# Fused attention and a four-expert mixture: the second stage's query tiles start at 0, 64, 192, 320 and 448

## The chip, the cores and the metric

One Trainium2 chip, one core. The metric is the device time of one execution in microseconds (us). A program is launched once; its inputs and its output lie in the chip's memory (HBM).

## What is computed

Eight batches of 576 tokens. The first stage is an attention with eight heads of width 64 (heads 0 to 3 look at the last 32 tokens, heads 4 to 7 at every 32nd token). Its result x (576 x 512 in each batch) goes to the second stage: four experts, each a causal attention over all 576 tokens with a head of width 64, and for each token the two experts with the largest gate value are summed with their weights.

```python
logits = x @ w_gate
topk = np.argpartition(-logits, K, axis=-1)[..., :K]      # K = 2 of 4 experts
w = np.exp(sel - max); w /= w.sum()
for e in range(4):
    q, k, v = x @ wq[e], x @ wk[e], x @ wv[e]
    scores = (q @ k.T) / 8, keys after the query masked
    a = softmax(scores)
    out += (w of expert e, 0 where not chosen) * (a @ v @ wo[e])
```

## The kernel before

Experts go in pairs: `ep` is 0 or 1, and `a` (0 or 1) is the expert within the pair. Expert a of a pair lies in partitions 64a to 64a+63 of the projected queries and keys, so that the two experts' score products run side by side in the two halves of TensorE's rows.

Each operation of the program is made by `op(kind, engines, key, fn, r, w, mode)`. The operations are numbered in the order in which they are made (2573 of them), and `schedule()` issues them in the order of the written list `ORDER`. `SECOND` names those that go to the second of their allowed engines (ScalarE or VectorE for copies), and `FILL` puts idle 128-column products ahead of some early operations. TensorE thus works through its operations in the order of that list, and waits wherever an operand isn't there. `mode` is the way in which the array is divided for an operation; TensorE's operations have these:

- 128x128: projections (`pj`, L906 and L918), values (`vp`, L853), output products (`yp`, L1110), scores of the short tile (`s2_4`, L972)
- 64x128 (two halves of the rows): scores (`s2`, L992), transposes of the probabilities (`t2`, L1048)
- 128x64 (two halves of the columns): probabilities by values (`acc`, L1081)
- 64x32, 64x64 and 32x64: the first stage's products (L628, L642, L736, L755) and one small product of the gate (`gate4`, L836)

`attend(b, ep, qk, un, key)` does one pair of experts of one batch for one of two units of query tiles. The tiles start at 0, 128, 256, 384 and 512; unit 0 has the first three, unit 1 the fourth and the fifth, which is 64 queries tall. For a tile of 128 queries: `s2` makes the scores against all keys up to the tile's end, as three products for each expert (high by high, low by high, high by low parts); `max2` (VectorE) masks, finds the maximum and writes the scores to SBUF; `exp2` (ScalarE) exponentiates and sums; after the unit's last tile, `recip2` (VectorE) takes reciprocals, and `scale2` (GpSimd) multiplies the probabilities by reciprocal and gate weight. The 64-row tile holds both experts in one 128-row tile: `qd` is a block-diagonal copy of its queries, `s2_4` makes 576 columns in two products of 288 columns each (three passes each), and `scale2_4` scales them. `t2` then transposes 64 x 128 blocks (50 of these in the two units of a pair: 12 + 12, 8 + 8 + 10), `t2_out` copies them from PSUM to `th` (10 copies), and `acc` multiplies them with the values: 768 columns for each expert in unit 0, 832 in unit 1. `oh` and `ol` split the sum into two parts. `out_tile` makes one 128 x 512 tile of the output from both pairs (six products of 512 columns), copies it and stores it.

The first stage (`stage1`) and the second stage of different batches are interleaved by `ORDER`. Units 1 of an even batch and of the odd one after it are done late, after both have units 0.

Of the kernel before, what the change touches and what calls it, by code (L numbers as in the profile page):

```python
# [20 lines left out]
def attention_moe_kernel(  # L21
# [28 lines left out]
    QT = [(0, 128), (128, 128), (256, 128), (384, 128), (512, 64)]  # L50
    UNITS = [[0, 1, 2], [3, 4]]
    NT = len(QT)
    HS = S // 2
    NV = E * D + E
# [26 lines left out]
    class Ring:  # L81
# [32 lines left out]
    }  # L114
    ORDER = [
# [242 lines left out]
    for m in (m_loc, m_str, m_cau, m_last):  # L358
        nc.vector.memset(m, 0.0)
# [15 lines left out]
    for hf in range(2):  # L375
        keep(m_last[64 * hf:64 * hf + 64, HS - 64:], [[-1, 64]], 0, 1)

# [816 lines left out]
```

## Time and profile before

| what | value |
|---|---|
| time, median of 3 runs | 445.7 us (442.08 to 446.44) |
| profiled execution: time | 446.46 us |
| profiled execution: span of the core's instructions | 444.7 us |
| mean granted TensorE clock in the span | 0.992 |
| TensorE matmuls busy | 427.8 us (96% of the span) |
| VectorE / ScalarE / GpSimd busy | 345.9 / 269.5 / 221.0 us |

The profiled execution is at the upper end of the three timed runs, 0.76 us above their median; 1.76 us of its time lie outside the span. Busy time is the union of the instructions' times on an engine. A matmul's time is from its issue to its last result, so consecutive ones overlap: what one costs is read from the starts of two that follow each other, not from its duration.

### The profile page before, as it was taken

To read this page: it belongs to the slowest core of one execution; us is meant where nothing else is said; L and a number is where in the kernel's file an instruction comes from. 1 tells how busy PE (TensorE), PEld (TensorE's weight loads), DVE (VectorE), ACT (ScalarE), POOL (GpSimd) and SP (SyncE) were. 2 spreads that over 40 slices of the span, in tenths; PEclk is the share of its full clock that TensorE was granted. 3 is DMA by queue.
4 is the path that set the end of the run, shared out by engine and by line. 5 is a ranking of instruction groups with operands and counts; after the bars stand their busy time and mean duration, and the time that the engine had idled before them with its cause. 6 is when DMAs were issued, how large, how long until landed. Compare 5 with 4: busy or idle time off the path is not lost.

```text
span 444.7 us, 19093 instructions
## 1 busy us (share of the span) xinstructions
PE 427.8 (96%) x7716; PEld 382.8 (86%) x7716; DVE 345.9 (78%) x1104; ACT 269.5 (61%) x848; POOL 221.0 (50%) x408
## 2 busy tenths in 40 slices
PE   7899998999989999999999999999999999999996
PEld 6788987977879998997889898998879998998874
DVE  6878899889985977789997768796998868555651
ACT  4475537676675757556486475557565577645662
POOL 4556641777534633376536552346833754405440
PEclk9989999999999999999999999999999999999999
DMA  6756656636545604545625336215832211001113
GB/s 178 188 140 151 126 116 125 125 58 107 113 103 118 124 23 105 113 90 118 117 50 131 68 59 124 61 33 107 193 76 73 67 43 54 1 1 58 45 68 118
DMA packets 156272, 41.89 MB, mean 94 GB/s; under 512 B 145976, under 2 KB 149432, under 8 KB 156184
## 3 DMA queue, kind: packets, MB, share of 16 engines
q1 hardware_dynamic: 156184, 40.67, 41.3%
q8 instruction: 61, 1.00, 0.9%
q14 instruction: 27, 0.22, 0.2%
HBM read 31.20 MB, written 9.44 MB: 91 GB/s over the span
## 4 chain that ended last, share of the span: by engine, by line
PE 85%; DVE 4%; SPq 3%; issue 3%; DMA 2%; ACT 2%; POOL 1%; POOLq 0%; DVEq 0%; ACTq 0%
PE bank L906 20%; PE bank L1110 12%; PE bank L853 10%; PE bank L1081 9%; PE bank L992 7%; PE bank L1048 6%; PE bank L736 4%; PE bank L972 3%; PE bank L755 3%; PE bank L628 3%; PE bank L642 3%; DMA v<-in_v_dram 1%; PE bank L706 1%; PE bank L816 1%; SPq L549 1%
## 5 line engine op out<-in xcount | busy, mean ns | idle before, releaser
L1029 POOL TENSOR_SCALAR p<-p,st,wt 128x512 f32<-128x512 f32 (+3 forms) x128 | 76.6, 610 | 42.4 <-DVE st L1013 17.2
L1004 ACT ACTIVATE p<-p,st 128x384 f32<-128x384 f32 (+3 forms) x128 | 71.8, 569 | 0.7 <-DVE st L999 0.6
L999 DVE CUSTOM_DVE_ANT_0 p<-bank,m_cau 128x128 f32<-128x128 f32 (+3 forms) x128 | 57.2, 481 | 6.6 <-PE bank L992 5.7
L927 ACT CAST qk<-bank 128x288 fp32r<-128x288 f32 x64 | 25.2, 400 | 56.3 <-PE bank L906 49.8
L338 ACT COPY th<-bank 128x384 f32<-128x384 f32 (+2 forms) x119 | 46.1, 436 | 13.5 <-PE bank L1048 9.8
L523 DVE STREAM_TRANSPOSE qkt<-nat 128x576 f32<-128x576 f32 x48 | 47.7, 1006 | 1.5 <-DMA nat<-in_k_dram 1.2
L1081 PE MATMUL bank<-th,vs 128*64 128x192 f32 (+4 forms) x512 | 48.5, 337 | 0.0
L1081 PEld LDWEIGHTS bank<-th,vs 128*64 128x64 f32 x512 | 33.6, 137 | 13.9 <-issue 6.9
L718 ACT CAST xh<-bank 128x128 fp32r<-128x128 f32 (+4 forms) x112 | 28.7, 322 | 21.6 <-PE bank L736 10.4
L720 DVE TENSOR_TENSOR xl<-bank,xh 128x128 fp32r<-128x128 f32 (+4 forms) x112 | 32.1, 324 | 12.4 <-ACT xh L718 11.7
L929 DVE TENSOR_TENSOR qkl<-bank,qk 128x288 fp32r<-128x288 f32 x64 | 27.8, 444 | 12.6 <-ACT qk L927 12.5
L1048 PE MATMUL bank<-ident,p 64*128 64x64 f32 x800 | 36.5, 226 | 0.5 <-DVE xl L720 0.3
L853 PE MATMUL bank<-wl_v,xh 128*128 128x260 f32 x128 | 36.2, 283 | 0.6 <-issue 0.6
L1048 PEld LDWEIGHTS bank<-ident,p 64*128 64x128 f32 x800 | 32.3, 139 | 5.3 <-issue 1.6
L853 PE MATMUL bank<-wh_v,xh 128*128 128x260 f32 x128 | 36.4, 284 | 0.0
L853 PE MATMUL bank<-wh_v,xl 128*128 128x260 f32 x128 | 36.2, 283 | 0.0
L906 PE MATMUL bank<-xh,wh_k 128*128 128x288 f32 x120 | 36.1, 301 | 0.0
L906 PE MATMUL bank<-xh,wh_q 128*128 128x288 f32 x120 | 35.9, 299 | 0.0
L906 PE MATMUL bank<-xl,wh_k 128*128 128x288 f32 x120 | 35.8, 299 | 0.0
L906 PE MATMUL bank<-xh,wl_k 128*128 128x288 f32 x120 | 35.8, 298 | 0.0
L906 PE MATMUL bank<-xl,wh_q 128*128 128x288 f32 x120 | 35.7, 298 | 0.0
L906 PE MATMUL bank<-xh,wl_q 128*128 128x288 f32 x120 | 35.5, 296 | 0.0
(182 smaller groups left out, 1254.4 us busy)
## 6 DMA issues: line engine op xcount, KB each, us to landing
out_dram<-ys SPq DMA_DIRECT2D x32, 256.0 KB
nat<-in_q_dram SPq DMA_DIRECT2D x96, 72.0 KB
nat<-in_k_dram SPq DMA_DIRECT2D x96, 72.0 KB
v<-in_v_dram SPq DMA_DIRECT2D x96, 40.0 KB
v<-in_v_dram SPq DMA_DIRECT2D x48, 54.0 KB
v<-in_v_dram SPq DMA_DIRECT2D x32, 48.0 KB
v<-in_v_dram SPq DMA_DIRECT2D x32, 45.0 KB
out_dram<-ys SPq DMA_DIRECT2D x8, 128.0 KB
```

What stands on the lines that cost most here:

```text
L338: (nc.scalar.copy if e == "ACT" else nc.vector.tensor_copy)(dst, src)
L523: op("tq", {"DVE": 0.66 if local else 1.11}, k0 - 13, lambda e, x=x: nc.vector.transpose(turned(qkt.t, x), raw(x) if local else raw(x).rea ...
L720: op("xl", {"DVE": dve(n_)}, key + 0.5, lambda e, s_=s_, x_=x_: nc.vector.tensor_sub(x_(xl.t), s_(xa.t), x_(f(xh.t))), r=[xa, xh[u]], w=[x ...
L853: nc.tensor.matmul(vp.t[:, :NV], xx.t[:, t0:t0 + 128], ww.t[:, kt, :], start=i == 0, stop=i == 11)
L906: nc.tensor.matmul(pj.t[:, :HS], ww.t[:, kt, ep * 128:(ep + 1) * 128], xx.t[:, c], start=i == 0, stop=i == 11)
L992: nc.tensor.matmul(sp[a].t[:, :nk], x.t[r, 0, q0:q0 + 128], y.t[r, 1, :nk], start=i == 0, stop=i == 2)
L999: lambda e, sp=sp, p=p, a=a, nk=nk, ci=ci: nc.vector.tensor_tensor_reduce(out=p.t[:, a, :nk], in0=sp[a].t[:, :nk], in1=m_cau[:, S - nk:], ...
L1004: op("exp2", {"ACT": 0.285 + 0.00084 * nk}, k_ + 1, lambda e, p=p, a=a, ci=ci, nk=nk: nc.scalar.activation(p.t[:, a, :nk], p.t[:, a, :nk], ...
L1029: lambda e, p=p, a=a, ci=ci, t=t, nk=nk: nc.gpsimd.tensor_scalar(p.t[:, a, :nk], p.t[:, a, :nk], st.t[:, 20 + ci + a:21 + ci + a], wt.t[:, ...
L1048: nc.tensor.transpose(tp[hf].t[:, 64 * c:64 * c + 64], src, ident[r, r])
L1081: nc.tensor.matmul(acc.t[o, c0:c0 + cn], vw, th[a].t[:, s0:s0 + cn], start=j == 0, stop=j == idx[-1], skip_group_check=True)
L1110: nc.tensor.matmul(yp.t[:, :DM], xx.t[:, c0:c0 + 128], ww.t[:, ep, :], start=i == 0, stop=i == 5)
```

## The change

1. The query tiles of the second stage start at 0, 64, 192, 320 and 448 (`AQ`): the 64-row tile that holds both experts is now the first, and needs 64 key columns only. The four others have 128 queries and 192, 320, 448 and 576 key columns. The last is done in two pieces of 288 columns, since a PSUM bank holds 512, in the 64x128 mode.
2. A tall tile ends 64 keys past a multiple of 128. These last 64 keys count for the lower 64 rows only. `scale2` leaves them out; `scale2w` (GpSimd) makes a product of reciprocal and gate weight, `scale2x` (GpSimd) scales the 64-row piece into a tile of its own (`xt`), `t2` transposes it as an extra block in one half of the rows (four in a pair of experts), and `t2_ext` copies it (six more copies in a pair).
3. `acc` takes its operands from one `th` tile for both experts (three buffers of 2 x 640 columns in place of four of 832). Unit 0 has pieces of 256, 64, 192 and 64 columns, unit 1 seven of 128 and two of 64.
4. The gate weights are copied to the new tiles' rows (`gate_q0`, `gate_ql`, `gate_qh`, `gate_q4`); `gate4`, `gate5` and `gate6` are gone.
5. The last output tile is made, copied and stored in two halves of 256 columns.
6. `ORDER`, `SECOND` and `FILL` are new (2804 operations). The lists are not shown here.

```diff
+    AQ = [(0, 64)] + [(64 + 128 * i, 128) for i in range(4)]
...
+    TH = fixed("th", [128, 2, TW], NTH, value=lambda t: [t[64:, :, :64], t[64:, :, TW - 64:]])
...
-            op("gate4", {"PE": 0.07}, key + 1.1, turn, r=[w4], w=[w4s], mode=MQ)
...
+            if t == 0:
+                sp = RB.new(f"s2_{n}_{t}")
+
+                def mm0(e, sp=sp):
+                    for i, (l, r) in enumerate(((0, qk), (1, qk), (0, qk.lo))):
+                        nc.tensor.matmul(sp.t[:, :64], qk.d.t[:, l], r.t[:, 1, :64], start=i == 0, stop=i == 2)
+
+                op("s2_0", {"PE": 0.25}, k_, mm0, r=[qk.d, qk[1, 0], qk.lo[1, 0]], w=[sp, p], mode=M128)
...
-                    def mml(e, sp=sp, c0=c0, q0=q0):
-                        for i, (l, r) in enumerate(((0, qk), (1, qk), (0, qk.lo))):
-                            nc.tensor.matmul(sp.t[:, :HS], qk.d.t[:, l], r.t[:, 1, c0:c0 + HS], start=i == 0, stop=i == 2)
...
+            cuts = [(0, nk)] if nk <= 512 else [(0, HS), (HS, nk)]
+            for hh, (c0, c1) in enumerate(cuts):
...
+                            nc.tensor.matmul(sp[a].t[:, :cn], x.t[r, 0, q0:q0 + 128], y.t[r, 1, c0:c0 + cn],
+                                             start=i == 0, stop=i == 2)
...
+            op("scale2x", {"POOL": 0.36}, kk + 0.3 * (t - idx[0]) + 0.2,
+               lambda e, p=p, t=t, x=x: nc.gpsimd.tensor_tensor(
+                   xt.t[64:, x].rearrange("p (a c) -> p a c", a=2), p.t[64:, :, 128 * t:128 * t + 64],
+                   st.t[64:, 27 + 2 * x:29 + 2 * x].unsqueeze(2).to_broadcast([64, 2, 64]), ALU.mult),
+               r=[p["x", 0], p["x", 1], st["w"]], w=[xt[x]])
...
+            work = [(0, [(0, [(2, 0, 1), (1, 0, 0), (2, 0, 0)], ()), (1, [(2, 1, 1), (1, 1, 0), (2, 1, 0), (0, 0, 0)], (1, 2))])]
...
+            work = [(3, [(0, [(3, a, j) for a in range(2) for j in range(3)], (3,))]),
+                    (4, [(1, [(4, 0, j) for j in range(4)], ()), (2, [(4, 1, j) for j in range(4)], (4,))])]
...
+                    for c, t in enumerate(ext, nb):
+                        r = slice(64, 128)
+                        nc.tensor.transpose(tp[1].t[:, 64 * c:64 * c + 64], xt.t[r, t - t0], ident[r, r])
...
+                jobs = [(0, 192, 64, 256, 0, 0), (0, 1088, 0, 64, 0, 1), (1, 0, 128, 192, 0, 0), (2, TW - 64, 256, 64, 0, 0)]
...
+                jobs = [(j, 64 + 128 * j, 128 * x, 128, x, 0) for x in range(2) for j in range(3 + x)]
+                jobs += [(3 + x, TW - 64, 128 * x + 64, 64, x, 0) for x in range(2)]
...
+        cut = 2 if b == B - 1 and t == 3 else 1
```

## Rows read from the trace of the kernel before

**Rows 1.** The page's first part: busy time of each engine.

```profile
PE 427.8 (96%) x7716; PEld 382.8 (86%) x7716; DVE 345.9 (78%) x1104; ACT 269.5 (61%) x848; POOL 221.0 (50%) x408
```

**Rows 2.** A stretch: length, busy time (instructions) by engine, granted clock, DMA share, GB/s.

```profile
150.00:200.00 50.00, 50.00 (x783) 45.69 (x779) 40.02 (x134) 32.63 (x105) 23.42 (x49) 1.00 0.41 87
```

**Rows 3.** TensorE's three largest waits from 60 us on: in total, times, longest.

```profile
PE bank L628 <- issue: 3.4, 3, 1.7
PE bank L736 <- DMA v<-in_v_dram: 1.4, 2, 0.8
PE bank L642 <- issue: 1.2, 2, 0.8
```

**Rows 4.** Stretches of 75 to 80 us, columns as in rows 2.

```profile
75.00:78.00 3.00, 3.00 (x39) 2.91 (x39) 2.48 (x6) 0.18 (x2) 1.36 (x5) 0.64 0.75 124
78.00:80.00 2.00, 2.00 (x13) 2.00 (x13) 1.10 (x2) 1.75 (x6) 1.62 (x3) 0.69 0.49 77
```

**Rows 5.** Timeline of TensorE, output products around 103 us: start, us, instructions.

```profile
103.21 0.50 PE L1110 MATMUL bank<-wh_o,oh 128*128 128x512 f32 x1
103.55 0.40 PE L1110 MATMUL bank<-wh_o,ol 128*128 128x512 f32 x1
103.78 0.39 PE L1110 MATMUL bank<-wl_o,oh 128*128 128x512 f32 x1
...
104.46 0.39 PE L1110 MATMUL bank<-wl_o,oh 128*128 128x512 f32 x1
104.78 0.53 PE L1048 MATMUL bank<-ident,p 64*128 64x64 f32 x10
```

**Rows 6.** The chain that ended last, three pieces with `acc`: start, us, what.

```profile
200.32 1.47 PE bank L1081 x12
...
210.22 2.86 PE bank L1081 x32
...
377.26 1.57 PE bank L1081 x20
```

**Rows 7.** Timeline of TensorE: scores of the tall tiles, around 199 and 253 us.

```profile
198.26 0.49 PE L992 MATMUL bank<-qk 64*128 64x512 f32 x1
...
199.05 0.53 PE L1048 MATMUL bank<-ident,p 64*128 64x64 f32 x11
199.39 0.36 PE L992 MATMUL bank<-qk 64*128 64x256 f32 x1
...
199.83 0.27 PE L992 MATMUL bank<-qk 64*128 64x128 f32 x2
...
252.45 0.27 PE L992 MATMUL bank<-qk,qkl 64*128 64x128 f32 x2
252.56 0.28 PE L992 MATMUL bank<-qkl,qk 64*128 64x128 f32 x2
...
253.31 0.41 PE L1048 MATMUL bank<-ident,p 64*128 64x64 f32 x8
253.54 0.51 PE L992 MATMUL bank<-qk 64*128 64x384 f32 x2
...
254.16 0.55 PE L1048 MATMUL bank<-ident,p 64*128 64x64 f32 x10
```

**Rows 8.** Timeline of TensorE: scores of the short tile (60 us), idle products (5 us).

```profile
60.14 0.44 PE L972 MATMUL bank<-qk,qd 128*128 128x288 f32 x2
...
60.55 0.43 PE L972 MATMUL bank<-qk,qd 128*128 128x288 f32 x2
...
4.92 1.05 PE L301 MATMUL bank<-ident 128*128 128x128 f32 x8
5.81 0.60 PE L571 MATMUL bank<-ident,p 128*128 128x128 f32 x4
```

**Rows 9.** A group by line and form: count, busy us, mean ns, idle before.

```profile
L1092 ACT CAST ofh<-bank 128x64 fp32r<-128x64 f32 x16 | 3.5, 218 | 5.8 <-PE bank L1081 5.4 <-DVE ol L1094 0.4
```

**Rows 10.** Timeline of ScalarE's last copy: start, us, waited before.

```profile
441.01 0.58 ACT L338 COPY ys<-bank 128x512 f32<-128x512 f32 x1 [0.73 <-PE bank L1110]
```

More of the change, by code (lines that the diff above doesn't have):

```diff
@@ L356, in attention_moe_kernel @@
     m_cau = const.tile([128, S], F32, name="m_cau")
-    m_last = const.tile([128, HS], F32, name="m_last")
-    for m in (m_loc, m_str, m_cau, m_last):
+    m_one = const.tile([128, 64], F32, name="m_one")
+    for m in (m_loc, m_str, m_cau, m_one):
         nc.vector.memset(m, 0.0)
@@ L413, in load_weights @@
         W[name] = [fixed(f"w{i}_{name}", [128, nk, n], 1, F32R).new("") for i in "hl"]
-        wide = [(P2[2] if name == "v" else TH).new(f"wst_{name}{i}") for i in range(0 if name == "o" else 2)]
+        if name in "qk":
+            wst = TH.new(f"wst_{name}")
+            wide = [wst[0], wst[1]]
+        else:
+            wide = [P2[2].new(f"wst_{name}{i}") for i in range(0 if name == "o" else 2)]
         hi, lo = W[name]
@@ L466, in stage1 @@
         k0 = T * (b + 0.25 * hp) if b else 2.0 + 4.0 * START.index(hp)
-        nat = (P2[3] if b == 0 and local else NAT).new(f"nat_{n}")
+        nat = (P2[4] if b == 0 and local else NAT).new(f"nat_{n}")
         qkt, st = QKT.new(f"qkt_{n}"), ST1.new(f"st1_{n}")
@@ L776, in stage1 @@
                r=[x[3]] if local else [x[i] for i in range(3)], w=[f_[hp, b % 2]])
-    VS = [fixed(f"vs{i}", [128, NT, NV], 1, value=lambda t, i=i: [t[64 - 64 * i:128 - 64 * i, NT - 1, :]]) for i in range(2)]
+    VS = [fixed(f"vs{i}", [128, NT, NV], 1, value=lambda t: [t[64:, NT - 1, :]]) for i in range(2)]
     LGT = ring("gt", [128, NT - 1, E, E], 1)
@@ L859, in values2 @@
         gates("", lambda: vs.t[:, :NT - 1, E * D:], [vs[t] for t in range(NT - 1)], WT[b], NT - 1, key + 4 * step)
+        wt, wq_ = WT[b], WQ[b]
+        for i in range(2):
+            op("gate_q0", {"ACT": 0.12, "DVE": 0.1}, key + 4 * step + 0.6, lambda e, i=i: copy(
+                e, wq_.t[64 * i:64 * i + 64, 0, :2], wt.t[:64, 0, i:E:2]), r=[wt], w=[wq_[0]])
+        op("gate_ql", {"ACT": 0.12, "DVE": 0.1}, key + 4 * step + 0.6, lambda e: copy(
+            e, wq_.t[:64, 1:], wt.t[64:, :, :E]), r=[wt], w=[wq_[1]])
+        op("gate_qh", {"ACT": 0.12, "DVE": 0.1}, key + 4 * step + 0.6, lambda e: copy(
+            e, wq_.t[64:, 1:NT - 1], wt.t[:64, 1:, :E]), r=[wt], w=[wq_[2]])
     def gates(tag, lg, src, wt, nt, k_):
@@ L954, in attend @@
         p2 = {}
-        ncol = {0: 6, 1: 3}[un]
+        xt = XT.new(f"xt_{n}_{un}")
+        col = {0: 0, 1: 1, 2: 3, 3: 0, 4: 2}
+        ncol = {0: 5, 1: 4}[un]
         for t in idx:
-            q0, m = QT[t]
+            q0, m = AQ[t]
             nk = q0 + m
@@ L986, in attend @@
-            sp = [RB.new(f"s2_{n}_{t}_{a}") for a in range(2)]
-            def mm(e, sp=sp, q0=q0, nk=nk):
-                for i, (x, y) in enumerate(((qk, qk), (qk.lo, qk), (qk, qk.lo))):
-                    for a in range(2):
-                        r = slice(64 * a, 64 * a + 64)
-                        nc.tensor.matmul(sp[a].t[:, :nk], x.t[r, 0, q0:q0 + 128], y.t[r, 1, :nk], start=i == 0, stop=i == 2)
-            op("s2", {"PE": {128: 0.355, 256: 0.39, 384: 0.525, 512: 0.7}[nk]}, k_, mm,
-               r=[x[0, u] for u in us for x in (qk, qk.lo)] + [x[1, u] for u in range((nk - 1) // HS + 1) for x in (qk, qk.lo)],
-               w=[*sp, p[0], p[1]], mode=MR)
@@ new lines, in attend, with mm @@
+            us = {(q0 // HS), (q0 + m - 1) // HS}
+            cuts = [(0, nk)] if nk <= 512 else [(0, HS), (HS, nk)]
+            for hh, (c0, c1) in enumerate(cuts):
+                sp = [RB.new(f"s2_{n}_{t}_{a}{hh}") for a in range(2)]
+                cn = c1 - c0
+                def mm(e, sp=sp, q0=q0, c0=c0, cn=cn):
+                    for i, (x, y) in enumerate(((qk, qk), (qk.lo, qk), (qk, qk.lo))):
+                        for a in range(2):
+                            r = slice(64 * a, 64 * a + 64)
+                            nc.tensor.matmul(sp[a].t[:, :cn], x.t[r, 0, q0:q0 + 128], y.t[r, 1, c0:c0 + cn],
+                                             start=i == 0, stop=i == 2)
+                op("s2", {"PE": {192: 0.37, 320: 0.46, 448: 0.62, 288: 0.42}[cn]}, k_ + 0.4 * hh, mm,
+                   r=[x[0, u] for u in us for x in (qk, qk.lo)] +
+                   [x[1, u] for u in range(c0 // HS, (c1 - 1) // HS + 1) for x in (qk, qk.lo)],
+                   w=[*sp, p[0], p[1]], mode=MR)
+                end = c1 == nk
+                for a in range(2):
+                    to = ci + a if end else 6 + a
+                    op("max2", {"DVE": 0.08 + 0.00104 * cn}, k_ + 0.5 + 0.4 * hh,
+                       lambda e, sp=sp, p=p, a=a, c0=c0, c1=c1, nk=nk, to=to, hh=hh: nc.vector.tensor_tensor_reduce(
+                           out=p.t[:, a, c0:c1], in0=sp[a].t[:, :c1 - c0], in1=m_cau[:, S - nk + c0:S - nk + c1], scale=-SCALE,
+                           scalar=st.t[:, 6 + a:7 + a] if hh else BIG, op0=ALU.add, op1=ALU.min, accum_out=st.t[:, to:to + 1]),
+                       r=[sp[a]] + ([st["h", a]] if hh else []), w=[p[a], st[t, a] if end else st["h", a]])
@@ L1072, in av @@
         def av(e):
-            for j in range(idx[-1] + 1):
+            if un == 0:
+                jobs = [(0, 192, 64, 256, 0, 0), (0, 1088, 0, 64, 0, 1), (1, 0, 128, 192, 0, 0), (2, TW - 64, 256, 64, 0, 0)]
+            else:
+                jobs = [(j, 64 + 128 * j, 128 * x, 128, x, 0) for x in range(2) for j in range(3 + x)]
+                jobs += [(3 + x, TW - 64, 128 * x + 64, 64, x, 0) for x in range(2)]
+            for i, (j, s0, c0, cn, x, one) in enumerate(jobs):
                 for a in range(2):
@@ L1101, in out_tile @@
         c0 = 0 if last else QT[t][0]
-        yp, ys = RB.new(f"yp_{b}_{t}"), YS.new(f"ys_{b}_{t}")
+        ys = YS.new(f"ys_{b}_{t}")
         src = [OF[b // 2, ep] if last else O[b, ep] for ep in range(2)]
-        need = [x[i] for pair in src for x in pair for i in ((0, 1) if last else (int(t > 2),))]
-        def mm(e):
-            i = 0
-            for ep in range(2):
-                for xx, ww in split3(src[ep], W["o"]):
-                    nc.tensor.matmul(yp.t[:, :DM], xx.t[:, c0:c0 + 128], ww.t[:, ep, :], start=i == 0, stop=i == 5)
-                    i += 1
@@ L1113, in out_tile @@
-        op("yp", {"PE": 6 * 0.229}, key, mm, r=need + wbufs("o"), w=[yp, ys], mode=M128)
-        op("yp_out", either(DM), key + 0.5, lambda e: copy(e, ys.t, yp.t[:, :DM]), r=[yp], w=[ys])
-        def store(e):
-            t0 = QT[t][0]
-            if last:
-                nc.sync.dma_start(out[b - 1, t0:, :], ys.t[:64, :])
-                nc.sync.dma_start(out[b, t0:, :], ys.t[64:, :])
-            else:
-                nc.sync.dma_start(out[b, t0:t0 + 128, :], ys.t)
-        op("store", {"SP": 0.5}, key + 1, store, r=[ys], dmas=[(0.4, 0.4)] * 2 if last else [(0.4, 0.8)])
+        need = [x[i] for pair in src for x in pair for i in ((0, 1) if last or t == 2 else (int(t > 2),))]
@@ new lines, in out_tile, with mm, store @@
+        cut = 2 if b == B - 1 and t == 3 else 1
+        n_ = DM // cut
+        for h in range(cut):
+            yp = RB.new(f"yp_{b}_{t}" + "b" * h)
+            c = slice(h * n_, (h + 1) * n_)
+            def mm(e, yp=yp, c=c):
+                i = 0
+                for ep in range(2):
+                    for xx, ww in split3(src[ep], W["o"]):
+                        nc.tensor.matmul(yp.t[:, :n_], xx.t[:, c0:c0 + 128], ww.t[:, ep, c], start=i == 0, stop=i == 5)
+                        i += 1
+            op("yp", {"PE": 6 * 0.229 / cut}, key + h, mm, r=need + wbufs("o"), w=[yp, ys[h]], mode=M128)
+            op("yp_out", either(n_), key + h + 0.5, lambda e, yp=yp, c=c: copy(e, ys.t[:, c], yp.t[:, :n_]), r=[yp], w=[ys[h]])
+            def store(e, c=c):
+                t0 = QT[t][0]
+                if last:
+                    nc.sync.dma_start(out[b - 1, t0:, :], ys.t[:64, :])
+                    nc.sync.dma_start(out[b, t0:, :], ys.t[64:, :])
+                else:
+                    nc.sync.dma_start(out[b, t0:t0 + 128, c], ys.t[:, c])
+            op("store", {"SP": 0.5}, key + h + 1, store, r=[ys[h]], dmas=[(0.4, 0.4)] * 2 if last else [(0.4, 0.8)])
```

198 lines of the change are left out of this document (99 added, 99 removed), and 314 rows, old and new, of tables (ORDER, SECOND).

## The prediction

> **What bounds the kernel now.** I read the page's first part first: TensorE has matmuls under way for 427.8 of 444.7 us, and no other engine is over 78% [rows 1]. Then the stretches: from 150 to 200 us TensorE is busy for the whole 50.00 us, at a granted clock of 1.00, that is 2.4 GHz [rows 2]. So the kernel is bound by TensorE's own list of operations, and a change counts by what it adds to or takes from that list. The 16.9 us in which TensorE has nothing are the rest. Of the waits after 60 us the three largest groups make 6.0 us [rows 3], most of them for the first stage's products. The longest, 1.7 us at 73 us, has a sequel: in the 5 us from 75 us on the granted clock is 0.64 and 0.69, a mix of 2.4 and 1.2 GHz, which loses 3 x 0.36 + 2 x 0.31 = 1.7 us more [rows 4]. Together 7.7 us after 60 us can be won or lost by an order.
>
> Durations of matmuls don't help here, since they overlap. I read starts: what an operation costs is the time from its first start to the next operation's first start.
>
> **Changes of mode, the largest term.** An output product (mode 128x128) steps 0.23 us from one 512-column product to the next; its first step, where the operation before had another mode, is 0.34, and its last step, to a transpose in mode 64x128, 0.32 [rows 5]. So a change costs some 0.09 us at the exit and 0.11 at the entry. The products of probabilities and values say the same: unit 0 alone takes 1.47, unit 1 alone 1.57, and both back to back, with one change fewer, 2.86: 0.18 us a change [rows 6]. I numbered the operations as the source makes them (2573 and 2804, the lengths of the two lists) and went through both lists by `mode`. Before, 152 neighbours on TensorE differ in mode; after, 195. Up to the last first-stage product of batch 1 the counts are 32 and 31, so all 43 more lie in the part where TensorE hardly waits: most are between 64x128 (scores, transposes) and 128x128. Bounds: 0.09 (only the exit counts) gives 3.9 us, 0.20 gives 8.6. I take 0.17, near the 0.18 measured directly: **+7.3 us**.
>
> The Trainium skill says that changing the tiling mode drains TensorE ("TensorEngine Tiling (Array Packing)", Key Properties). It gives no time; the rows above do.
>
> **Scores.** For a pair of experts before: 128 columns cost about 0.37 (three pairs of products, 0.11 from pair to pair, and a little at the start), 256 cost 0.44, 384 cost 0.62, 512 cost 0.79 [rows 7], and the short tile twice 0.41 [rows 8]: 3.04 us. After, between these rows: 192 columns 0.40, 320 columns 0.53, 448 columns 0.70, and 288 columns twice 0.485: 2.60. The short tile's three products of 64 columns, full array, have no row. From below, three times 0.06 (a 64-column transpose at 0.029 us, 8 in 0.23 [rows 7], doubled) gives 0.18; from above, the 0.37 of the 128-column tile. The nearest row is the idle products with 128 columns on the full array, 8 in 0.89 us, 0.11 each [rows 8]: 0.33 us. After: 2.93, a gain of 0.11; less rounding I take 0.1 a pair, times 16 pairs: **-1.6 us**; bounds -4.2 and -0.3.
>
> **Transposes.** Before 50 in two units, at 0.029 us each where they alternate between the row halves: 1.45 us a pair [rows 7]. After, 42 alternate (1.22), and four extra blocks use one half only. Two that alternate take 0.058 together, so one half alone is ready for the next after at most that: 4 x 0.058 = 0.23. The sum is 1.45 again: **0**; if the lone blocks cost 0.029, -1.9 us.
>
> **Probabilities by values.** 768 + 832 columns for each expert before; after 256 + 64 + 192 + 64 = 576 and 7 x 128 + 2 x 64 = 1024: again 1600. 20 instructions in place of 12, with 64 more columns, cost 0.10 us more [rows 6], and 64 columns at 1.47 / 768 a column are 0.12, so instructions are nearly free. For ten more pairs of them I take 0.03 us: **+0.5 us**; from below 0.
>
> **The other engines.** GpSimd gets two `scale2w` and four `scale2x` a pair and loses 512 columns of `scale2`; it is at 50%. VectorE and ScalarE get six copies and one maximum more a pair, at about 0.22 us for 64 columns [rows 9]: 16 x 7 x 0.22 = 25 us over two engines, which brings VectorE from 346 to about 360 of 445 us. The gate's copies for the new rows replace copies for the old ones. All this is covered by TensorE's work between a unit's last scores and its first transposes. Adding up TensorE's durations along the two lists, that cover is at the median 14 us in unit 0 in both lists, and in unit 1 it goes from 13 to 31 us; the chain of one unit (maximum, exponential, reciprocal, scaling) has some 5 us. If the cover were gone, each unit would wait its extra 1 us of GpSimd: 32 us, so this is worth watching. `gate4` goes: nothing. `FILL` issues 69 idle products in place of 52, all in the first 60 us, where TensorE waits anyway: 0, at most 17 x 0.11 = 1.9 us if they stand in the way. The first loads come in another order in the queue of SyncE; the weights' last piece is the 36th or 37th load in both, so I take nothing for it.
>
> **The end.** The last copy takes 0.58 us for 512 columns [rows 10]; with 256 columns it is some 0.2 us shorter, and the last store is half as large: **-0.3 us**, between 0 and -0.6.
>
> **Waits.** The new order sets more work between makers and takers: from the last product of the first stage to the first value projection of a batch it has 7 to 21 us of TensorE's work, against 3.5 to 7.7. I take it that half of the 7.7 us go: **-3.8 us**; bounds 0 and -13.7 (below).
>
> Sum against the profiled execution: 446.46 + 7.3 - 1.6 + 0 + 0.5 - 0.3 = 452.4, less 3.8 of waits = 448.6. The profiled execution was 0.76 above the median, so I forecast **447.8 us** against 445.7. That is within 1%, about what a measurement of this kernel can tell from no change (its three runs span 1%).
>
> **Rivals.**
>
> A. *The waits go altogether.* Of the 16.9 us without a matmul [rows 1], some 5 are the start and the end; the other 12 and the 1.7 of slow clock could all go, since makers and takers are further apart: 445.7 + 5.9 - 13.7 = 437.9. It beats 1% if more than 10.4 of the 13.7 go. For it: the longer cover. Against: some waits are for loads, which no cover within the list brings earlier.
>
> B. *The changes of mode cost nothing,* because they fall beside waits: 447.8 - 7.3 = 440.5. Against: they lie where TensorE is busy throughout [rows 2].
>
> C. *The waits stay* (slower). They stand before the first stage's products [rows 3], whose input passes through SyncE's queue and then VectorE's, in order; VectorE gets some 15 us more, queued ahead of the next batch's transposes. Then the sum has no gain to set against the changes of mode: 445.7 + 5.9 = 451.6. It is over 1% slower if less than 1.4 us of waits go.
>
> D. *Loading the stationary operand bounds the 64-column pieces* of probabilities by values (slower). Each pair has four such pieces instead of one, six more pairs of instructions; were each bound at 0.11 us, as the 128-column scores are [rows 7], and not at the 0.05 us of its columns, that is 16 x 6 x 0.06 = 5.8 us: 453.6. Against: unit 1's own 64-column piece fits the column price [rows 6].
>
> The Trainium skill has a rule on D's side: loading stationary columns takes their number over 1.2 GHz ("TensorE: Matmul & The Clock Gate", LDWEIGHTS), by which two loads of 64 columns take an estimated 0.107 us. The trace has transposes with 128 stationary columns every 0.029 us [rows 7], which is faster than that rule.
>
> **How the numbers follow.** Forecast 0.42 (its own range 444 to 452), A 0.20, B 0.08, C 0.23, D 0.07. Over 1% faster is below 441.2: most of A, half of B, a little of the forecast's lower bounds (scores at -4.2): 0.23. Over 1% slower is above 450.2: three quarters of C, most of D, the forecast's upper bounds: 0.29. Within: 0.48. The range from 440 to 453.5 leaves out half of A and half of D, and the far ends of C.
>
> **What would show it.** The changes of mode: the first steps of output products at 0.34 and last ones at 0.32, more often; more back-to-back pieces of few operations in the chain. Scores: `s2_0` at 0.33 us, the 288-column pieces at 0.485. Extra transposes: 0.058 from start to start. `acc`: the 12 + 20 instructions become 16 + 36, at about 1.13 and 1.90 us between changes. Waits: the sum after 60 us, and whether the clock still falls at 75 us. The prediction is wrong if waits change by more than I allow, either way, or if `s2_0` or the lone transposes cost twice what I took.

## The result, and the profile after

The changed kernel takes 450.96 us (median of 11 runs, 448.30 to 454.89), the kernel before 446.42 us in the same session (11 runs, 442.08 to 449.90): a ratio of 1.0133, 95% interval 1.0102 to 1.0164. That is 1.3% slower, inside the range, 3.2 us above the forecast and just beyond the 1% that I called no change. Ratios, here and below, compare the means of the runs at the higher clock alone; of the kernel before, three runs (448.8 to 449.9 us) are left out for that, and so its ratio is more than that of the two medians. The profiled execution of after is at 450.96 us, 4.5 us above that of before.

The page of after: busy times, granted clock in 40 slices, the queue that brings instructions, and the shares of the chain that ended last. Behind it that last line for before.

```profile
PE 437.2 (97%) x8056; PEld 395.6 (88%) x8056; DVE 366.4 (82%) x1210; ACT 277.0 (62%) x906; POOL 245.4 (55%) x499
...
PEclk9999998999999999999999999999999999999999
...
q8 instruction: 63, 1.03, 1.0%
...
PE 77%; POOL 12%; DVE 5%; issue 3%; ACT 1%; DMA 0%; SPq 0%; POOLq 0%; DVEq 0%; ACTq 0%
```

```profile
PE 85%; DVE 4%; SPq 3%; issue 3%; DMA 2%; ACT 2%; POOL 1%; POOLq 0%; DVEq 0%; ACTq 0%
```

TensorE still sets the time: it gained 9.4 us of busy time where the span gained 4.5 [rows 1]. VectorE gained 20.5 us and GpSimd 24.4. The chain now runs through GpSimd for 12% of the span, 1% before. That is a path and not a price: TensorE works meanwhile, and its waits for GpSimd below are 1.0 us.

TensorE's waits from the first value projection (56 us) to its last product, the whole answer; it stands against [rows 3].

```profile
PE bank L667 <- issue: 1.4, 1, 1.4
PE bank L653 <- issue: 1.3, 1, 1.3
PE bank L1093 <- POOL p L1061: 0.7, 2, 0.5
PE bank L653 <- DVE sel L913: 0.6, 1, 0.6
PE bank L761 <- DVE pt L721: 0.3, 1, 0.3
PE bank L992 <- POOL qd L961: 0.3, 1, 0.3
PE bank L780 <- DMA v<-in_v_dram: 0.2, 1, 0.2
```

These make 4.8 us; the same view of before, from 51 us on, makes 6.9 us: the 6.0 of [rows 3] and two more lines.

```profile
PE bank L853 <- issue: 0.6, 1, 0.6
PE bank L1048 <- DVE xl L720: 0.3, 1, 0.3
```

So the waits that this view names went down by 2.1 us. All of that is in the waits that it puts down to nothing ("issue"): 5.2 us before, 2.7 after. Waits for another engine or a transfer went from 1.7 to 2.1.

Three stretches of after: 71 to 75, 75 to 78 and 150 to 200 us, columns as in [rows 2].

```profile
71.00:75.00 4.00, 2.70 (x91) 2.24 (x90) 2.31 (x9) 3.90 (x17) 0.24 (x1) 0.67 0.82 149
75.00:78.00 3.00, 3.00 (x26) 2.54 (x24) 2.77 (x13) 0.38 (x1) 0.00 (x0) 0.87 0.72 110
...
150.00:200.00 50.00, 49.92 (x986) 44.93 (x978) 42.92 (x144) 32.74 (x113) 26.05 (x54) 1.00 0.41 87
```

The loss of clock that follows the first long wait is still there [rows 4], somewhat earlier: 4 x 0.33 + 3 x 0.13 = 1.7 us, as before. In steady work TensorE is as full as before [rows 2].

The chain, start and length of some pieces: the start of the kernel, probabilities by values (L1148), and VectorE's and GpSimd's part between two units.

```profile
1.42 2.50 PE bank L321 x10
3.92 3.99 PE bank L1202 x10
...
407.88 0.57 POOL p L1061
408.49 0.46 PE bank L1093 x8
...
413.69 1.14 PE bank L1148 x16
...
415.87 1.93 PE bank L1148 x36
```

And the same view of before at its start:

```profile
0.92 0.28 DVE p1l L346
1.21 0.04 issue
1.25 3.83 PE bank L1130 x10
```

The warm-up (L1202, before L1130) starts first in before; in after five idle products (ten matmuls, L321) stand ahead of it, for 2.5 us.

Timeline of TensorE in after: an output product between operations of other modes, the work of one unit's change-over, two pieces of 288 columns, and the last copy:

```profile
210.93 0.50 PE L1182 MATMUL bank<-wh_o,oh 128*128 128x512 f32 x1
211.27 0.39 PE L1182 MATMUL bank<-wh_o,ol 128*128 128x512 f32 x1
...
212.19 0.40 PE L1182 MATMUL bank<-wl_o,oh 128*128 128x512 f32 x1
212.52 0.46 PE L1093 MATMUL bank<-ident,p 64*128 64x64 f32 x8
...
408.49 0.46 PE L1093 MATMUL bank<-ident,p 64*128 64x64 f32 x8 [0.45 <-POOL p L1061]
408.76 0.39 PE L1012 MATMUL bank<-qk 64*128 64x320 f32 x1
408.79 0.28 PE L1096 MATMUL bank<-ident,xt 64*128 64x64 f32 x2
...
409.50 0.41 PE L992 MATMUL bank<-qk,qd 128*128 128x64 f32 x2
409.74 0.28 PE L992 MATMUL bank<-qkl,qd 128*128 128x64 f32 x1
409.85 0.48 PE L1182 MATMUL bank<-wh_o,oh 128*128 128x512 f32 x1
410.17 0.39 PE L1182 MATMUL bank<-wh_o,ol 128*128 128x512 f32 x1
...
422.26 0.38 PE L1012 MATMUL bank<-qk 64*128 64x288 f32 x2
...
422.74 0.30 PE L1012 MATMUL bank<-qk 64*128 64x288 f32 x2
...
423.15 0.41 PE L1093 MATMUL bank<-ident,p 64*128 64x64 f32 x8
...
445.98 0.37 ACT L358 COPY ys<-bank 128x256 f32<-128x256 f32 x1 [0.84 <-PE bank L1182]
```

With a change of mode on either side, an output product's first step is 0.34 and its last 0.33, as in [rows 5]; 17 first steps of after have it, 13 of before. The short tile's three products take 0.35 us from their first start to the output product's, the change of mode ahead of them among it; the two that have their own mode on both sides take 0.25. That is not all that they cost. The output product at 409.85 us has the short tile's mode, so no change stands between them, and yet its first step is 0.32 in place of 0.23. In 13 of the 16 pairs of experts an operation in that mode follows the short tile, and each time its first step is about 0.09 us longer than elsewhere: 1.1 us in all.

The two lone transposes of 408.79 us start 0.06 apart (one takes 0.22, both 0.28), while the alternating ones make two in that time; the scores behind them start 0.03 us before the first of them. The first piece of 288 columns, behind transposes, takes 0.48 us, the second, behind the first, 0.41. The last copy takes 0.37 us in place of 0.58 [rows 10].

**Where the 4.5 us come from.** I matched each operation of the two lists to its instructions, took for each kind the typical time from its first start to the next operation's first start, and separated what a change of mode adds. By these prices the list takes 411.8 us before and 413.2 after. What an operation takes beyond its price I call excess: waits, slow clock, small stalls.

| part | before | after |
|---|---|---|
| first operation of the list starts (profiled trace) | 1.25 | 3.71 |
| first value projection starts | 51.01 | 55.96 |
| ... of which more list work placed ahead of it | | +3.0 |
| first value projection to the last product's end | 389.96 | 389.94 |
| excess after 50 us, total | 12.2 | 13.8 |
| ... in steps with over 0.4 us | 10.6 | 6.9 |
| ... in steps with 0.12 to 0.4 us | 2.5 | 5.4 |
| ... the rest, below 0.12 us either way | -1.0 | 1.5 |
| from the last product's end to the end of the span | 3.76 | 3.3 |

From the first value projection on both kernels take the same time. There the list of after is 1.4 - 3.0 = -1.6 us, and its excess 1.6 us larger. Since prices go from first start to first start, the 1.1 us by which the short tile delays its follower stand in this excess, in the row of the rest; without them it grew by 0.5 us.

### The profile page after: what moved, and what is told of

The parts are those of the page before. It is cut to its first block, busy times and chain, and to the rows that moved or that the text cites. A ratio compares the mean times of both kernels' runs of the same rounds, so it can differ in the third digit from the quotient of the medians.

```text
span 449.2 us, 20034 instructions
## 1 busy us (share of the span) xinstructions
PE 437.2 (97%) x8056; PEld 395.6 (88%) x8056; DVE 366.4 (82%) x1210; ACT 277.0 (62%) x906; POOL 245.4 (55%) x499
## 3 DMA queue, kind: packets, MB, share of 16 engines
q8 instruction: 63, 1.03, 1.0%
## 4 chain that ended last, share of the span: by engine, by line
PE 77%; POOL 12%; DVE 5%; issue 3%; ACT 1%; DMA 0%; SPq 0%; POOLq 0%; DVEq 0%; ACTq 0%
PE bank L930 16%; PE bank L1148 10%; PE bank L1182 9%; PE bank L1012 7%; PE bank L869 7%; POOL p L1061 5%; PE bank L1093 5%; PE bank L653 4%; PE bank L761 3%; PE bank L321 3%; PE bank L780 3%; PE bank L667 3%; POOL xt L1067 2%; PE bank L942 2%; PE bank L731 2%
## 5 line engine op out<-in xcount | busy, mean ns | idle before, releaser
L1061 POOL TENSOR_SCALAR p<-p,st,wtq 128x384 f32<-128x384 f32 (+3 forms) x128 | 77.4, 613 | 30.9 <-DVE st L1037 14.6
L1028 ACT ACTIVATE p<-p,st 128x192 f32<-128x192 f32 (+3 forms) x128 | 78.5, 616 | 8.0 <-DVE st L1023 7.4
L1023 DVE CUSTOM_DVE_ANT_0 p<-bank,m_cau 128x320 f32<-128x320 f32 (+3 forms) x128 | 58.1, 474 | 7.3 <-PE bank L1012 6.5
L358 ACT COPY th<-bank 128x256 f32<-128x256 f32 (+4 forms) x164 | 49.4, 330 | 18.5 <-PE bank L1096 6.9
L1148 PE MATMUL bank<-th,vs 128*64 128x128 f32 (+3 forms) x832 | 49.9, 272 | 0.0
L1148 PEld LDWEIGHTS bank<-th,vs 128*64 128x64 f32 x832 | 43.3, 137 | 6.2 <-issue 0.9
L743 ACT CAST xh<-bank 128x160 fp32r<-128x160 f32 (+4 forms) x112 | 29.7, 322 | 29.7 <-PE bank L761 21.6
L694 POOL TENSOR_TENSOR p1l<-p1l,st 128x640 f32<-128x640 f32 (+1 forms) x18 | 20.4, 1143 | 39.2 <-DVE st L692 39.1
L745 DVE TENSOR_TENSOR xl<-bank,xh 128x160 fp32r<-128x160 f32 (+4 forms) x112 | 33.2, 321 | 5.8 <-ACT xh L743 5.2
L358 DVE COPY th<-bank 128x256 f32<-128x256 f32 (+4 forms) x92 | 31.1, 347 | 6.3 <-PE bank L1096 1.9
```

Of the source, the lines that this page charges most:

```text
L358: (nc.scalar.copy if e == "ACT" else nc.vector.tensor_copy)(dst, src)
L743: op("xh", {"ACT": act(n_) + 0.04 * (not local)}, key, lambda e, s_=s_, x_=x_: nc.scalar.copy(x_(xh.t), s_(xa.t)), r=[xa], w=[xh[u]])
L745: op("xl", {"DVE": dve(n_)}, key + 0.5, lambda e, s_=s_, x_=x_: nc.vector.tensor_sub(x_(xl.t), s_(xa.t), x_(f(xh.t))), r=[xa, xh[u]], w=[x ...
L1023: lambda e, sp=sp, p=p, a=a, c0=c0, c1=c1, nk=nk, to=to, hh=hh: nc.vector.tensor_tensor_reduce(out=p.t[:, a, c0:c1], in0=sp[a].t[:, :c1 - ...
L1028: op("exp2", {"ACT": 0.285 + 0.00084 * nk}, k_ + 1, lambda e, p=p, a=a, ci=ci, nk=nk: nc.scalar.activation(p.t[:, a, :nk], p.t[:, a, :nk], ...
L1061: lambda e, p=p, a=a, ci=ci, t=t, nk=nk - 64: nc.gpsimd.tensor_scalar(p.t[:, a, :nk], p.t[:, a, :nk], st.t[:, 20 + ci + a:21 + ci + a], wq ...
```

## The experiments

All were timed in five rounds beside the kernel before. The theory was that the changes of mode cost what I summed, and that what the new order was to give back in waits was not given back. The rivals were the layout's longer chain on VectorE and GpSimd, the idle products, or something in TensorE's own stream.

**The layout alone.** Tiles as changed, the operations placed as the kernel before places theirs, with its idle products and its share of the copies between engines (`FILL` and `SECOND`, not shown):

```diff
-    ORDER = [44, 45, 0, 46, 51, 2, 1, 48, 54, 53, 50, 47, ...
+    ORDER = [1, 0, 2, 44, 8, 45, 3, 13, 12, 5, 88, 15, ...
```

> The new layout of the query tiles with all its new operations, in the order of the kernel before: each operation stands where its counterpart stood, new small operations right behind the one they depend on; the idle products at the start are those of the kernel before. Changes of mode on TensorE: 186 (152 before, 195 in the changed kernel). Theory (TensorE's own list sets the time; scores save 4.5 us, transposes 2.0, the end 0.5, values cost 0.6, a change of mode costs 0.17 us): -6.4 + 34 x 0.17 = -0.6 us, a ratio to the kernel before of 0.995 to 1.003. Rival (the layout itself costs, through GpSimd's longer chain and the extra copies, whatever the order): 1.010 or more.

It took 590.43 us, ratio 1.3286 (1.3222 to 1.3350). TensorE's largest waits:

```profile
PE bank L1093 <- POOL p L1061: 44.7, 22, 5.3
PE bank L992 <- POOL qd L961: 10.4, 14, 2.8
PE bank L1148 <- ACT th L358: 4.9, 6, 1.3
```

Both expectations were far off in size. The transposes of a unit (L1093) wait 22 times, up to 5.3 us, for GpSimd's scaled probabilities. So the new layout has no use for the old places: there TensorE stands waiting for its chain, which the new order hides. The re-sorting moved operations of the other engines too, and the granted clock fell to 0.907 over the span (0.995 in after), so the 145 us more than before are a bound for this mechanism and not its price.

**The new order with fewer changes of mode.** An operation in the mode of the one before was pulled forward over up to 60 places, 162 changes in place of 195:

```diff
-        ..., 228, 315, 231, 1140, 233, 1156, 1152, 291, ...
+        ..., 1156, 1158, 1140, 1185, 1152, 228, 315, 231, ...
```

> The changed kernel, its order alone touched: from place 300 of the list on, an operation of TensorE is taken up to 60 places earlier where it has the mode of the one before it and its operands allow it. 162 changes of mode in place of 195. Theory (0.17 us a change): 5.6 us less than the changed kernel, a ratio to the kernel before of about 1.000 (0.996 to 1.005). Rival (changes of mode fall beside waits and cost little; the time comes from waits and the start): 1.010 to 1.016 as the changed kernel, or more.

594.95 us, ratio 1.3385 (1.3321 to 1.3450). The waits are spread over all lines; the largest:

```profile
PE bank L762 <- DMA v<-in_v_dram: 5.4, 1, 5.4
PE bank L1013 <- DVE st L1024: 4.8, 8, 1.1
```

Here 1156 of the 2804 places differ. The 33 changes that it saved are worth 5.6 us at 0.17; it lost 144 us, with the granted clock at 0.880 over the span. The run says nothing on the price of a change; it shows that a rule which moves that many operations without regard to the other engines costs far more than it saves.

**The kernel before with more changes of mode.** Neighbours up to 12 places apart swapped, 160 of 2573 places, 196 changes in place of 152:

```diff
-        ..., 382, 1243, ..., 1303, 1304, 200, 415, 1323, ...
+        ..., 1243, 382, ..., 415, 1303, 1304, 200, 1383, ...
```

> The kernel before, its order alone touched: neighbouring operations of TensorE, at most 12 places apart, are exchanged where that adds changes of mode: 196 in place of 152, with the same operations. Theory (0.17 us a change): +7.5 us, a ratio of 1.012 to 1.020. Rival (a change costs little when TensorE's next operation waits anyway): under 1.006.

459.36 us, ratio 1.0327 (1.0283 to 1.0370), more than expected. In its trace the list by the same prices, with the changes of mode measured in it, takes 419.2 us, 7.4 more than before: 0.17 us for each of 44 changes, as forecast. The figure can be seen in one kind: an output product takes 1.39 to 1.40 us between operations of its own mode and 1.58 to 1.59 between others, in before, in after and here. The rest of what it lost after 50 us, 6.3 us of excess, lies mainly in waits that the swaps brought: after the first value projection the named waits for engines and transfers are 9.6 us in place of 1.7, and those put down to nothing 2.1 in place of 5.2. Two of the groups:

```profile
PE bank L1084 <- ACT th L341: 1.3, 1, 1.3
PE bank L1051 <- DVE xl L723: 1.1, 1, 1.1
```

**The new order with fewer idle products.** 20 are issued in place of 52, none ahead of the warm-up:

```diff
-        0: 5, 3: 1, 13: 6, 46: 4, 51: 2, 56: 2, 76: 7, 89: 1, 96: 5, 124: 4, ...
+        13: 3, 46: 2, 51: 1, 56: 1, 76: 3, 96: 2, 124: 2, ...
```

> The changed kernel with fewer idle products in the first 60 us: none ahead of the warm-up, half of the others (20 in place of 52 that are issued; the kernel before issues 29). Theory (they stand in the way at the start, 0.22 us each): 2 us less than the changed kernel, a ratio to the kernel before of 1.006 to 1.011. Rival (they fill waits only, and hold the clock): the same 1.013 as the changed kernel, or slower, with a granted clock under 0.9 somewhere in the first 60 us.

455.24 us, ratio 1.0246 (1.0203 to 1.0288): slower than after, with a clock of 1.000 over the profiled span. The first value projection starts 1.55 us earlier (54.41), but from there to the last product it takes 395.3 us in place of 389.9. Its largest waits:

```profile
PE bank L654 <- issue: 4.2, 5, 1.7
PE bank L668 <- issue: 3.1, 3, 1.6
```

Neither theory had this. After the first value projection the waits put down to nothing are 7.3 us, against 2.7 in after, though nothing there was edited. What did change is the position of every later instruction in TensorE's stream. 32 products fewer are 128 matmuls and loads fewer (x7992 in place of x8056, for matmuls and for loads). TensorE's instructions come over queue q8: 63 packets of 1.03 / 63 MB = 16 KB for 16,112 matmuls and loads, 256 to a packet; I call a packet's worth of them an instruction page. So all page ends had moved by half a page. The next eight kernels test that.

**As many instructions, narrower.** The 32 products that were left out come back 16 columns wide, those ahead of the warm-up behind it; then 32 and 64 more of them (half a page, a whole page), and 32 in the kernel before:

```diff
+                for _ in range(o.narrow):
+                    nc.tensor.matmul(bank[:, :16], ident, ident[:, :16], start=True, stop=True)
```

> The changed kernel with 32 of its 52 idle products made 16 columns wide in place of 128, and the five ahead of the warm-up moved behind it: as many TensorE instructions as the changed kernel, in the same places of the stream from the warm-up on. Theory (TensorE waits where the next page of 256 instructions is not there in time, so the places of the page ends decide, and the five products ahead of the warm-up cost about 2.4 us): TensorE starts at 1.3 us in place of 3.7, the first value projection near 54 us, waits put down to nothing stay near the changed kernel's 4.3 us, ratio to the kernel before 1.004 to 1.009. Rival (fewer wide idle products are what cost e4_after_fewer_fills its time): ratio 1.020 to 1.028, as there.

> e5_after_narrow_fills with 32 more narrow idle products in the first 50 us: 128 more TensorE instructions, half a page, in a stretch where TensorE waits for loads anyway. Theory (place of the page ends): all later page ends lie half a page elsewhere, as in e4_after_fewer_fills, waits put down to nothing 8 to 12 us, ratio 1.018 to 1.028. Rival (the place of the pages does not matter): within 0.3% of e5_after_narrow_fills.

> e5_after_narrow_fills with 64 more narrow idle products in the first 50 us: 256 more TensorE instructions, one whole page, so that all later page ends lie at the same operations as in e5_after_narrow_fills. Theory (place of the page ends): within 0.4% of e5_after_narrow_fills, ratio 1.004 to 1.012, under e6_after_narrow_half though it has more added. Rival (added products cost by their number): twice the distance of e6_after_narrow_half from e5_after_narrow_fills.

> The kernel before with 32 narrow idle products (16 columns) added in the first 50 us: 128 more TensorE instructions, half a page; nothing else differs. Theory (place of the page ends): the waits put down to nothing, 6.1 us before, change by 2 us or more in either direction, and the time with them, ratio outside 0.996 to 1.004. Rival (the place of the pages does not matter): ratio 0.998 to 1.003.

**The same with the columns kept.** Idle products of 128 columns cut in two or three, so that columns stay and instructions are added:

```diff
-                for _ in range(o.fill):
-                    nc.tensor.matmul(bank[:, :128], ident, ident, start=True, stop=True)
+                for j in range(o.fill):
+                    for a, z in CUTS[o.split[j]] if j < len(o.split) else CUTS[1]:
+                        nc.tensor.matmul(bank[:, a:z], ident, ident[:, a:z], start=True, stop=True)
```

> The changed kernel with 32 of its 52 idle products cut in two of 64 columns: 128 more TensorE instructions (half a page), the same columns, so that the clock of the first stage should stay at 1.00, which the narrow products of e6_after_narrow_half and e7_after_narrow_page did not keep. Theory (the place of the page ends decides what TensorE waits after the first value projection): from the first value projection to the last product 392.5 to 396 us in place of 389.9, waits put down to nothing at other lines, ratio to the kernel before 1.019 to 1.030. Rival (the place of the pages does not matter): 389.5 to 390.5 us, ratio 1.010 to 1.017.

> The changed kernel with the same 32 idle products cut in three: 256 more TensorE instructions (one whole page), the same columns. Theory (place of the page ends): all ends lie at the operations of the changed kernel again, first value projection to last product 389 to 391 us, ratio 1.010 to 1.018, under e9_after_split_half though twice as many instructions are added. Rival (more instructions cost by their number): above e9_after_split_half.

> The kernel before with its 29 idle products cut in two or three: 128 more TensorE instructions (half a page), the same columns. Theory (place of the page ends): first value projection to last product 392 to 393.5 us in place of 390.0 as in e8_before_half, which lost 4.5 us more in the first stage through its added products; ratio 1.004 to 1.009. Rival (what e8_before_half lost was the added products alone): 390 us, ratio 0.998 to 1.003.

> The kernel before with 16 of its 29 idle products cut in two: 64 more TensorE instructions (a quarter of a page). Theory (place of the page ends): other waits put down to nothing than the 6.1 us of before, by over 2 us in either direction, and with them the time: ratio 0.990 to 0.996 or 1.004 to 1.010; below 0.996 it would beat both kernels. Rival (no matter where): 0.998 to 1.003.

What they gave. The third column is the place of the page ends against the kernel it was made from; "projection" is the start of the first value projection, "from there" the time to the last product, "issue" the waits put down to nothing in that part, "all" all waits named in it; the last four from the profiled execution, in us.

| kernel | ratio to before | pages | projection | from there | issue | all |
|---|---|---|---|---|---|---|
| after | 1.0133 (1.0102 to 1.0164) | | 55.96 | 389.9 | 2.7 | 4.8 |
| e5_after_narrow_fills | 1.0138 (1.0107 to 1.0170) | same | 54.96 | 390.7 | 2.6 | 5.3 |
| e7_after_narrow_page | 1.0753 (1.0712 to 1.0793) | one page on | 84.86 | 388.4 | 2.6 | 4.5 |
| e10_after_split_page | 1.0447 (1.0413 to 1.0482) | one page on | 71.06 | 392.3 | 3.3 | 5.9 |
| e4_after_fewer_fills | 1.0246 (1.0203 to 1.0288) | half a page | 54.41 | 395.3 | 7.3 | 9.7 |
| e6_after_narrow_half | 1.0550 (1.0509 to 1.0591) | half a page | 72.22 | 393.5 | 7.2 | 8.8 |
| e9_after_split_half | 1.0394 (1.0354 to 1.0435) | half a page | 63.82 | 393.7 | 6.7 | 8.9 |
| before | 1 | | 51.01 | 390.0 | 5.2 | 6.9 |
| e8_before_half | 1.0148 (1.0110 to 1.0186) | half a page | 55.51 | 392.6 | 4.6 | 9.4 |
| e11_before_split_half | 1.0218 (1.0173 to 1.0264) | half a page | 56.74 | 391.5 | 3.8 | 8.1 |
| e12_before_split_quarter | 1.0102 (1.0072 to 1.0132) | a quarter | 54.21 | 388.4 | 5.4 | 7.1 |

*The total times are spoiled as a test.* The added products stand in a first stage with no room for them: they delay the first value projection by 3 to 29 us (e5 adds none). I had taken narrow products to be cheap, and they are not. Two rows, 16 columns in e6_after_narrow_half and 64 in e9_after_split_half:

```profile
44.82 2.75 PE L327 MATMUL bank<-ident 128*128 128x16 f32 x24
```

```profile
36.35 2.62 PE L328 MATMUL bank<-ident 128*128 128x64 f32 x22
```

An idle product is two matmuls, and each takes 0.112 us from start to start whether it has 128 columns [rows 8], 64 or 16. So 64 matmuls more are some 7.2 us, and e9_after_split_half starts its first value projection 7.9 us later; 128 more are 14.3, and in e10_after_split_page it is 15.1. In e6 and e7 the clock fell too. The stretch from 30 to 40 us in e6_after_narrow_half, and in e5_after_narrow_fills below it:

```profile
30.00:40.00 10.00, 10.00 (x178) 9.72 (x180) 4.26 (x10) 2.40 (x6) 1.46 (x2) 0.50 0.30 65
```

```profile
30.00:40.00 10.00, 8.26 (x321) 7.47 (x322) 8.98 (x24) 4.99 (x16) 5.18 (x7) 1.00 0.65 148
```

A granted clock of 0.50 is 1.2 GHz; TensorE was busy throughout, and there a matmul of 16 columns takes 0.21 us. So the totals of e6, e7, e9 and e10 went past all that I expected, and e7 and e10 came out above e6 and e9 where I expected them below. The total of e5 missed both of its expectations: it gained nothing by its earlier start.

*What is left is the part after the first value projection*, where the kernels of one family hold the same operations. In the family of after it separates: pages in the same place 388.4 to 392.3 us and 2.6 to 3.3 us of "issue" waits; pages half a page off 393.5 to 395.3 us and 6.7 to 7.3. The means differ by 394.2 - 390.3 = 3.8 us, the "issue" waits by 7.1 - 2.8 = 4.3. One whole page more brings the waits back to where they were, which a price on the number of instructions would not. In the family of before it does not separate: "issue" 5.2, 4.6 and 3.8, 5.4, and the times follow other waits. There both e8 and e12 missed their expectation of a change of 2 us in these waits, and e11's 391.5 us lies between its two expectations (392 to 393.5, and 390). In the family of after, e9 is where the theory put it, and e10 1.3 us above its range. The times come from one execution each, and the three runs of e11_before_split_half in its ratio spread from 453.7 to 457.6 us, so single distances of 2 us mean little.

The places themselves are the stronger evidence. For each wait of 0.5 us or more that is put down to nothing, after the first value projection, the number that the next instruction has among TensorE's matmuls and loads:

```
after                       3219 9289
e5 (same pages)             3219 9289
e7 (one page on)            3475 9545
e10 (one page on)           3475 6760 9545
e4 (half a page back)       3219 4739 6250 6502 9287 12332
e6 (half a page on)         6507 6759 9544 10559 11067 12589
e9 (half a page on)         6507 6759 9544 10559 12589
before                      3217 5497 8288 9042 10809
e8 (half a page on)         9294 10809 12328 13081
e11 (half a page on)        9294 10809 12329 13081
e12 (a quarter on)          3217 5497 10809 12327
```

If such a wait belonged to an operation, adding 128 instructions ahead of it would raise its number by 128. The numbers stay, or move by whole pages: 9289 and 9545 are 256 apart, so are 3219 and 3475. They all fit one division into pages: divided by 256 they leave 145 to 147 at 3217 to 3475, 121 at 5497, 71 to 78 at 9287 to 9545, 57 at 10809 and 25 at 13081, in both families, a fall of one in some 80, as instructions not counted here share the pages. The instruction at a number is another one: at 9287 to 9289, after and e4_after_fewer_fills hold operations 128 instructions apart. One such wait in each, from the timeline, after first:

```profile
231.03 0.65 PE L667 MATMUL bank<-qkt,nat 64*64 64x54 f32 x28
233.08 1.14 PE L667 MATMUL bank<-qkt,nat 64*64 64x54 f32 x62 [1.40 <-issue]
```

```profile
155.14 0.72 PE L668 MATMUL bank<-qkt,nat 64*64 64x54 f32 x31
157.42 0.49 PE L668 MATMUL bank<-qkt,nat 64*64 64x54 f32 x17 [1.56 <-issue]
```

In all of them the wait ends 1.0 to 1.6 us after a packet of q8 has ended. So these waits stand at page ends. A page holds some 7 us of work and only a few ends show such a wait; which ones seems to depend on what lies there: of the 43 listed 33 stand in the short products of the first stage, where 17 products take 0.49 us in the last row.

## Why the prediction was right or wrong

The time fell inside the range. The prices of scores and transposes were some 4 us too high together, waits and idle products some 6 us too low, so the nearness owes something to luck.

- *Changes of mode*, 43 x 0.17 = +7.3: right. The list has 7.4 us more of them, and e3_before_more_changes gave 7.4 for 44.
- *Scores*, -1.6: wrong in size. Measured -4.5 from first start to first start, -3.4 with the 1.1 us that the short tile costs the operation behind it. So its three products cost 0.25 + 0.09 us, and the 0.33 taken from the idle products was right. Wrong were the 288-column pieces, 0.42 on the whole and not 0.485: [rows 7] are scores behind transposes, which do cost 0.48, but the second piece stands behind the first and costs 0.40. (By the 0.37 that I named, the upper bound is -1.1 and not -0.3.)
- *Transposes*, 0: wrong in size. Measured -2.0, the bound for lone ones at 0.029, but not for that reason: lone ones stand 0.062 us apart, about the 0.058 that I took. Of the 64, 32 have an operation in their own mode behind them; as a rule it starts when it would have started without them, and they cost nothing there. The other 32 stand ahead of a change of mode and cost their 0.062, so that the mean is 0.03. I had left out what overlaps them.
- *Probabilities by values*, +0.5: right, +0.6. Between changes of mode 1.14 us for 16 instructions and 1.91 for 36, as written. Rival D falls: at its price each pair of experts would take 0.36 us more. By the rule of the Trainium skill on D's side ("TensorE: Matmul & The Clock Gate", LDWEIGHTS: columns over 1.2 GHz) 36 loads of 64 columns would take an estimated 1.92 us; the trace has 1.91 with a change of mode in it, so the loads are no slower than that estimate.
- *The end*, -0.3: right, -0.5.
- *Idle products*, 0, at most 1.9: the work ahead of the first value projection has 0.5 us less excess but starts 2.5 us later, so about 2.0 us, at the bound. I had taken all idle products to lie where TensorE waits anyway; five lie ahead of the warm-up, where it doesn't. The count was wrong too: 69 and 52 are what the lists ask for, but 52 and 29 are issued (104 and 58 matmuls), each two matmuls of 0.11, so that the bound should have been 23 x 0.22 = 5.1. How much of it counts at the end stays open. In e5_after_narrow_fills the warm-up starts at 1.25 us again, the first value projection comes 1.0 us earlier, and the time is the same (1.0138 against 1.0133).
- *Waits*, -3.8: the step that failed; they came out at about +0.5. Long stalls did fall by 3.7 us (10.6 to 6.9 of excess in steps over 0.4 us), but shorter ones in scores and transposes rose, and the excess after 50 us is 1.6 us larger, of which 1.1 are the short tile's. The waits for engines and transfers, which an order can shorten, were only 1.7 us before, and are 2.1 after. Most of what I had counted as theirs was "issue" at page ends, which I read as waits for the first stage's input [rows 3]. More work between makers and takers doesn't remove these; an order changes what lies at the page ends (e3_before_more_changes, with as many instructions as before, has 2.1 us of them in place of 5.2), and after happens to sit where they are small: half a page off they are some 4 us more.

Of the rivals, C has the outcome (the waits as a whole stay, a time of 451.6), with another mechanism: not VectorE's queue ahead of the first stage, but page ends and many short waits in the second stage. A and B are out: the waits did not go, and e3_before_more_changes paid for its changes. What the small waits are one by one stays open. The chain puts GpSimd (L1061) in their place, 12% of the span against 1% before, but in the waits it has only 0.7 us.

Whether the new tiles pay with a better order stays open too: the list without the changes of mode is 3.4 + 2.0 - 0.6 = 4.8 us shorter, and the 43 changes take 7.4. No version tried here beats the kernel before.

## What to carry to other kernels

Before a wait is credited to a better order, ask what ended it: one that the profile puts down to nothing, in a dense stretch of short products, can sit at the end of an instruction page and moves with the number of instructions ahead of it. A comparison of two orders then holds a few us of chance; shifting one of them by half a page, in a place that can bear it, shows how much. Price a short operation together with its neighbours: from first start to first start the three products of 64 columns seemed to cost 0.25 us, and the operation behind them paid the other 0.09; scores cost 0.08 more behind transposes than behind scores; a lone transpose cost 0.06 or nothing by what followed it. And a product of the full array is not made cheaper by making it narrower: idle ones took 0.11 us with 128 columns and with 16.

## What the runs showed of the hardware that I had not expected

- TensorE's instructions arrive in packets of 16 KB, 256 matmuls and loads each, and in dense short products TensorE stands still at their ends: 1.3 and 1.4 us in after, up to 2.0 in e12_before_split_quarter. Each such wait ended 1.0 to 1.6 us after the packet.
- Matmuls of idle products follow each other every 0.11 us whether 128, 64 or 16 columns wide (0.21 where the granted clock was 0.50, in e6_after_narrow_half). Behind the three 64-column products of the short tile, an operation in the same mode takes about 0.09 us more on its first step.
- Transposes on one row half alone start 0.06 us apart (408.79 us in after), alternating ones two in that time; an operation in the same mode starts beside a lone one without delay.
- In e6_after_narrow_half TensorE was busy for all of 30 to 40 us, and the granted clock was 0.50; in e5_after_narrow_fills it was busy for 8.26 of these 10 us, and the clock was 1.00.
